# Retention in 64-position chunks with 64x64 quarters in place of 128-position chunks

## The chip, the cores and the metric

The kernel runs on one core of one Trainium2 chip. The metric is device time in microseconds (us) of one launch. TensorE (PE) multiplies, VectorE (DVE), ScalarE (ACT) and GpSimd (POOL) work elementwise, SyncE (SP) issues the DMAs in program order. Each engine takes its instructions in the order in which they stand; only semaphores tie the engines together. Matmul results land in PSUM; here every PSUM tile is one bank (128 partitions x 512 float32).

## The reference

Four batches, 768 positions, 8 heads of 64 channels. A retention (linear attention with a decay per head) feeds a gated MLP:

```
gamma = 1.0 - 2.0 ** (-5.0 - np.arange(H))
for t in range(S):
    state = gamma[None, :, None, None] * state + np.einsum('bhd,bhe->bhde', k[:, :, t], v[:, :, t])
    y[:, :, t] = scale * np.einsum('bhd,bhde->bhe', q[:, :, t], state)

h = np.maximum(x @ w_in, 0.0)                 # x: y as (4, 768, 512), w_in 512 x 1024
u, v = (h[..., :d_ff // 2], h[..., d_ff // 2:])
v_n = (v - mean(v)) / np.sqrt(var(v) + 1e-06)
v_s = np.einsum('ts,bsd->btd', w_spatial, v_n) + b_spatial[None, :, None]
return (u * v_s) @ w_out                      # w_out 512 x 512
```

The weights `w_in` and `w_out` arrive in double precision.

## The kernel before

**MLP.** All its products are formed from operands that are split into a rounded high part and a remainder, three matmuls on the full 128x128 array for one product (`split3`, L316, and L414). For a batch: `mlp_v` (six tiles `v`, then `mlp_norm`), then eight items, each `mlp_u` (tile `u`), `mlp_spatial` (tile `sp`, which needs all six normalised tiles `vnh`, `vnl` of the batch) and `mlp_out` (tiles `o`). Weights are split on chip, block by block (`split_double`, tiles `da`, `df`: five DVE steps, two ACT, the rest DVE or POOL).

**Retention.** 24 chunks of 128 positions, six for a batch, numbered `g` through all batches (`c` is the place in the batch). Values are multiplied by a falling power of gamma (`scale_v`, POOL, L211), outputs by a rising one (`qd_t`, DVE, L279). `run(g)` does three things:

- `ret_out`: tile `x`, for each of four head pairs two matmuls of values on scores (L261: 128 rows of contraction, 64 columns of weights, 128 moving columns) and, from the second chunk of a batch, two of state on queries (L264, 64 rows). So the form of the matmul changes at every pair of heads.
- `score(g + 1)`: the scores of the next chunk. Chunks 0 to 8 (`scores_whole`, L244) form them from float32 operands and mask them on DVE (L248). Chunks 9 to 23 (`scores_split`, L224) use split operands stacked to 128 rows (`stack`: DVE, ACT and POOL work, L118, L202, L206), add two halves (L226 ACT, L227 DVE) and mask on POOL (L228).
- `ret_update`: tile `u`, keys on values (L289); the sum with the old state on DVE (L298), its decay on POOL (L299).

A float32 matmul shows in the profile as two passes, that of a split operand as one.

**Order.** The lists START, FIRST, REST and LAST give the order in which the parts are issued: START holds the splits of the weights, the whole first batch's retention (R0 to R5), R6 to R8 of the second batch, and the first `v` tiles; FIRST the items of batch 0 and R9 to R11; REST the items of a batch and the six chunks of the next batch; LAST the last eight items. A planner then sets each engine's order from these parts and from the pools: a tile of a pool can be written only when the tile that held its buffer is done with. The retention's PSUM pool has three banks for `s`, `x` and `u`.

Of the kernel before, what the change touches and what calls it, by code (L numbers as in the profile page):

```python
# [22 lines left out]
WHOLE = 9  # L23
# [7 lines left out]
START = (  # L31
# [3 lines left out]
)  # L35
FIRST = (
    "C7 L10 I0 L11 W01 W11 W21 C8 I1 W31 C9 I2 W51 T12 C10 W41 R9 T11 I3 C11 I4 Q11 R10 "
    "Q12 I5 I6 Q13 R11 V0 I7 V1 N0 V3 V2 N1 N2 T13 N3 V5 V4 N4 N5 O7"
)
REST = (  # L40
    "R0 Q2 T2 R1 I0 I1 Q3 T3 I2 R2 Q4 T5 I3 I4 R3 T4 Q5 I5 R4 Q6 T6 I6 Q7 T7 V0 I7 R5 V1 "
# [5 lines left out]
# Order in which the blocks of the weights in double precision are split, and how many of the  # L47
# residues are formed on the vector engine.
# [7 lines left out]
def tile_retention_gmlp(  # L56
    ctx: ExitStack,
    tc: tile.TileContext,
    qk: bass.AP,
    qT: bass.AP,  # L60
    kT: bass.AP,
    kv: bass.AP,
# [8 lines left out]
    cdecay: bass.AP,  # L71
# [5 lines left out]
    NG = kv.shape[0]  # L77
    NC = NG // B
    H, D = kv.shape[3], kv.shape[4]
    NP = H // 2  # L80
# [16 lines left out]
    mask_t = wpool.tile([P, P], F32, name="mask_t")  # L97
    vd_t = wpool.tile([P, H], F32, name="vd_t")
    qd_t = wpool.tile([P, NP, P], F32, name="qd_t")
    cd_t = wpool.tile([P, NP], F32, name="cd_t")  # L100
# [38 lines left out]
    def split_double(i):  # L139
# [3 lines left out]
        a = mpool.tile([P, DM], F32, tag="stage", name=f"da{i}")  # L143
# [19 lines left out]
    query = {}  # L163
    keys = {}
    kvs = {}
    stacked = {}
    scores = {}
    state = {}
    xhalf = {}

    def load_query(g):
        if g >= NG:
            return
        if g < WHOLE:
            t = rpool.tile([P, 2, NP, P], F32, tag="qk", name=f"qk{g}", bufs=3)
            load(t, qk[g])
            query[g] = [t[ROWS[h % 2], 0, h // 2] for h in range(H)]
            keys[g] = t[:, 1]
        else:
            kt = rpool.tile([P, NP, P], F32, tag="qk", name=f"k{g}", bufs=3)  # L180
            qt = rpool.tile([P, H, P], F32, tag="qk", name=f"q{g}", bufs=3)
            load(kt, kT[g - WHOLE])
            load(qt, qT[g - WHOLE])
            query[g] = [qt[ROWS[h % 2], h] for h in range(H)]
            keys[g] = kt
            stack(g, kt, qt)

    def load_value(g):
        if g >= NG:
            return  # L190
        kvs[g] = rpool.tile([P, 2, H, D], F32, tag="kv", name=f"kv{g}")
        load(kvs[g], kv[g])
        scale_v(g)

    def stack(g, kt, qt):
        k2 = mpool.tile([P, H, P], F32R, tag="raw", name=f"k2_{g}", bufs=3)
        q2 = [
            mpool.tile([P, NP, 2, P], F32R, tag="raw", name=f"q2_{g}_{i}", bufs=3)
            for i in range(2)
        ]  # L200
        for r in range(2):
            nc.scalar.copy(k2[ROWS[r], r::2], kt[ROWS[r]])  # L202
            residue(nc.vector, k2[ROWS[1 - r], r::2], kt[ROWS[r]], k2[ROWS[r], r::2])
        for i in range(2):
            qi = qt[:, NP * i : NP * i + NP]
            nc.scalar.copy(q2[i][:, :, 0], qi)  # L206
            residue(nc.gpsimd, q2[i][:, :, 1], qi, q2[i][:, :, 0])
        stacked[g] = (k2, q2)

    def scale_v(g):  # L210
        nc.gpsimd.tensor_tensor(  # L211
            kvs[g][:, 1], kvs[g][:, 1], vd_t[:, :].unsqueeze(2).broadcast_to([P, H, D]), ALU.mult
        )

    def scores_split(g):
        k2, q2 = stacked.pop(g)
        ps = []
        for i in range(2):
            p = rpool.tile([P, NP, P], F32, tag="p", name=f"p{g}_{i}", bufs=3)
            for u in range(2):  # L220
                t = ps_r.tile([P, 2, 2, P], F32, tag="ret", name=f"s{g}_{i}_{u}")
                for w in range(2):
                    h = 2 * u + w
                    nc.tensor.matmul(t[:, w], k2[:, NP * i + h], q2[i][:, h], start=True, stop=True)  # L224
                low = rpool.tile([P, 2, P], F32, tag="low", name=f"lo{g}_{i}_{u}")
                nc.scalar.copy(low, t[:, :, 1])  # L226
                nc.vector.tensor_tensor(p[:, 2 * u : 2 * u + 2], t[:, :, 0], low, ALU.add)  # L227
            nc.gpsimd.affine_select(  # L228
                out=p,
                in_=p,  # L230
                pattern=[[0, NP], [1, P]],
                compare_op=ALU.is_ge,
                fill=0.0,
                base=0,
                channel_multiplier=-1,
            )
            ps.append(p)
        scores[g] = [ps[h // NP][:, h % NP] for h in range(H)]

    def scores_whole(g):  # L240
        ts = [ps_r.tile([P, NP, P], F32, tag="ret", name=f"s{g}_{r}") for r in range(2)]
        for h in range(H):
            r, hp = h % 2, h // 2
            nc.tensor.matmul(ts[r][:, hp], keys[g][ROWS[r], hp], query[g][h], start=True, stop=True)  # L244
        ps = []
        for r in range(2):
            p = rpool.tile([P, NP, P], F32, tag="p", name=f"p{g}_{r}", bufs=3)
            nc.vector.tensor_tensor(  # L248
                p, ts[r], mask_t[:, :].unsqueeze(1).broadcast_to([P, NP, P]), ALU.mult
            )  # L250
            ps.append(p)
        scores[g] = [ps[h % 2][:, h // 2] for h in range(H)]

    def ret_out(g):
        b, c = divmod(g, NC)
        ps = scores.pop(g)
        t = ps_r.tile([P, NP, P], F32, tag="ret", name=f"x{g}")
        for hp in range(NP):
            for r in range(2):
                h = 2 * hp + r  # L260
                nc.tensor.matmul(t[ROWS[r], hp], kvs[g][:, 1, h], ps[h], start=True, stop=(c == 0))  # L261
            if c > 0:
                for r in range(2):
                    nc.tensor.matmul(  # L264
                        t[ROWS[r], hp],
                        state[g][ROWS[r], hp],
                        query[g][2 * hp + r],
                        start=False,
                        stop=True,
                    )  # L270
# [8 lines left out]
        nc.vector.tensor_tensor(xf, t, qd_t, ALU.mult)  # L279
        nc.scalar.copy(xh[:, :, cols], xf)  # L280
        residue(nc.gpsimd, xl[:, :, cols], xf, xh[:, :, cols])

    def ret_update(g):
        c = g % NC
        if c == NC - 1:
            return
        t = ps_r.tile([P, 4, P], F32, tag="ret", name=f"u{g}")
        for h in range(H):
            nc.tensor.matmul(  # L289
                t[ROWS[h % 2], h // 2, :D], kvs[g][:, 0, h], kvs[g][:, 1, h], start=True, stop=True  # L290
            )
        st = rpool.tile([P, NP, D], F32, tag="st", name=f"st{g}")
        cd = cd_t[:, :].unsqueeze(2).broadcast_to([P, NP, D])
        if c == 0:
            nc.vector.tensor_tensor(st, t[:, :, :D], cd, ALU.mult)
        else:
# [243 lines left out]
```

## Time and profile before

| | |
|---|---|
| median of 3 runs | 451.26 us (450.74 to 451.58) |
| span of the profiled execution | 445.8 us; the runs are some 5.5 us longer than it, which lies around the span |
| PE, DVE, POOL, ACT busy | 429.1, 234.2, 217.6, 159.8 us |
| matmul passes | 2834, 1288 of them in the retention |
| first `sp` matmul of batch 0 | at 81.16 us |
| data moved by DMA | 45.23 MB |

A row of the PE timeline merges passes of one line; its start, set against the start of the next row, gives the time that the passes took, since the ends are modelled and overlap.

### The profile page before, as it was taken

To read this page: it belongs to the slowest core of one execution; us is meant where nothing else is said; L and a number is where in the kernel's file an instruction comes from. 1 tells how busy PE (TensorE), PEld (TensorE's weight loads), DVE (VectorE), ACT (ScalarE), POOL (GpSimd) and SP (SyncE) were. 2 spreads that over 40 slices of the span, in tenths; PEclk is the share of its full clock that TensorE was granted. 3 is DMA by queue.
4 is the path that set the end of the run, shared out by engine and by line. 5 is a ranking of instruction groups with operands and counts; after the bars stand their busy time and mean duration, and the time that the engine had idled before them with its cause. 6 is when DMAs were issued, how large, how long until landed. Compare 5 with 4: busy or idle time off the path is not lost.

```text
span 445.8 us, 7214 instructions
## 1 busy us (share of the span) xinstructions
PE 429.1 (96%) x2834; PEld 352.0 (79%) x2834; DVE 234.2 (53%) x397; ACT 159.8 (36%) x319; POOL 217.6 (49%) x228
## 2 busy tenths in 40 slices
PE   4998989989999999999999999999999999999995
PEld 2665657777899877887988877888879778999994
DVE  2899989883863556661423556652413534422122
ACT  2324234543434344641433433652423312411211
POOL 1457874695673627473724747365534522211110
PEclk8899999996999999999999999999999999999999
DMA  7846456434125320530213330342313000100102
GB/s 259 312 129 217 130 192 216 147 132 131 43 101 190 93 73 0 209 123 1 96 71 130 109 118 0 102 160 71 96 71 119 1 0 2 71 1 0 72 0 71
DMA packets 16881, 45.23 MB, mean 101 GB/s; under 512 B 2128, under 2 KB 4048, under 8 KB 16848
## 3 DMA queue, kind: packets, MB, share of 16 engines
q1 hardware_dynamic: 16848, 44.77, 29.7%
q8 instruction: 22, 0.36, 0.3%
q14 instruction: 11, 0.09, 0.1%
HBM read 38.48 MB, written 6.29 MB: 100 GB/s over the span
## 4 chain that ended last, share of the span: by engine, by line
PE 77%; DVE 10%; POOL 5%; issue 3%; DMA 3%; SPq 1%; ACT 0%; ACTq 0%; POOLq 0%; DVEq 0%
PE sp L316 22%; PE o L414 14%; PE u L316 14%; PE v L316 11%; PE x L261 6%; PE x L264 5%; PE s L224 3%; PE u L289 2%; DMA kv<-in_kv_dram 1%; DVE p L248 1%; DVE df L149 1%; DMA k<-in_kT_dram 1%; DVE da L151 1%; DVE da L147 1%; DVE da L150 1%
## 5 line engine op out<-in xcount | busy, mean ns | idle before, releaser
L118 POOL TENSOR_TENSOR gl<-t,gh 128x384 fp32r<-128x384 f32 x31 | 32.0, 1032 | 76.2 <-ACT gh L400 72.5
L316 PE MATMUL sp<-wsp_h,vnh 128*128 128x384 f32 x192 | 65.4, 341 | 0.0
L316 PE MATMUL sp<-wsp_l,vnh 128*128 128x384 f32 x192 | 65.0, 339 | 0.0
L316 PE MATMUL sp<-wsp_h,vnl 128*128 128x384 f32 x192 | 64.3, 335 | 0.0
L398 DVE TENSOR_TENSOR t<-sp,bsp_t 128x384 f32<-128x384 f32 (+1 forms) x34 | 17.9, 532 | 76.7 <-PE sp L316 74.3
L261 PE MATMUL x<-p,kv 128*64 128x128 f32 x384 | 45.0, 306 | 6.4 <-POOL kv L211 4.4
L118 POOL TENSOR_TENSOR xl<-xf,xh 128x512 fp32r<-128x512 f32 x24 | 35.0, 1460 | 25.5 <-ACT xh L280 23.3
L118 POOL TENSOR_TENSOR q<-q,q 128x512 fp32r<-128x512 f32 x30 | 41.1, 1380 | 11.9 <-ACT q L206 11.9
L316 PE MATMUL u<-xh,winu_h 128*128 128x384 f32 x128 | 43.9, 343 | 0.0
L261 PEld LDWEIGHTS x<-p,kv 128*64 128x64 f32 x384 | 22.0, 140 | 27.4 <-issue 19.1
L316 PE MATMUL u<-xh,winu_l 128*128 128x384 f32 x128 | 43.5, 340 | 0.0
L316 PE MATMUL u<-xl,winu_h 128*128 128x384 f32 x128 | 43.1, 337 | 0.0
L400 ACT CAST gh<-t 128x384 fp32r<-128x384 f32 (+1 forms) x34 | 16.6, 494 | 68.9 <-DVE t L399 67.8
L316 PE MATMUL v<-winv_h,xh 128*128 128x512 f32 x96 | 39.3, 411 | 0.0
L316 PE MATMUL v<-winv_h,xl 128*128 128x512 f32 x96 | 39.0, 406 | 0.0
L227 DVE TENSOR_TENSOR p<-s,lo 128x256 f32<-128x256 f32 x60 | 23.8, 419 | 28.5 <-ACT lo L226 28.3
L316 PE MATMUL v<-winv_l,xh 128*128 128x512 f32 x96 | 38.7, 404 | 0.0
L211 POOL TENSOR_TENSOR kv<-kv,vd_t 128x512 f32<-128x512 f32 x24 | 26.9, 1120 | 24.0 <-DMA kv<-in_kv_dram 17.9
L228 POOL TENSOR_SCALAR_AFFINE_SELECT p<-p 128x512 f32<-128x512 f32 x30 | 24.2, 808 | 28.8 <-DVE p L227 28.6
L414 PE MATMUL o<-wout_l,gh 128*128 128x512 f32 x96 | 37.5, 394 | 0.0
L316 PEld LDWEIGHTS sp<-wsp_h,vnh 128*128 128x128 f32 x192 | 36.0, 188 | 1.7 <-issue 0.7
L226 ACT COPY lo<-s 128x256 f32<-128x256 f32 x60 | 21.0, 374 | 45.6 <-PE s L224 40.3
(73 smaller groups left out, 878.6 us busy)
## 6 DMA issues: line engine op xcount, KB each, us to landing
kv<-in_kv_dram SPq DMA_DIRECT2D x24, 512.0 KB, 3.5
q<-in_qT_dram SPq DMA_DIRECT2D x15, 512.0 KB, 3.4
out_dram<-ot SPq DMA_DIRECT2D x23, 256.0 KB, 2.0
qk<-in_qk_dram SPq DMA_DIRECT2D x9, 512.0 KB, 5.4
k<-in_kT_dram SPq DMA_DIRECT2D x15, 256.0 KB, 3.6
wst<-in_w_sp_dram SPq DMA_DIRECT2D x12, 192.0 KB, 3.6
raw<-in_w_inv_dram SPq DMA_DIRECT2D x4, 512.0 KB, 6.6
raw<-in_w_inu_dram SPq DMA_DIRECT2D x4, 512.0 KB, 3.8
```

The costliest lines, as they stand in the source:

```text
L118: eng.tensor_tensor(out, whole, high.bitcast(F32), ALU.subtract)
L211: nc.gpsimd.tensor_tensor(kvs[g][:, 1], kvs[g][:, 1], vd_t[:, :].unsqueeze(2).broadcast_to([P, H, D]), ALU.mult)
L224: nc.tensor.matmul(t[:, w], k2[:, NP * i + h], q2[i][:, h], start=True, stop=True)
L226: nc.scalar.copy(low, t[:, :, 1])
L227: nc.vector.tensor_tensor(p[:, 2 * u : 2 * u + 2], t[:, :, 0], low, ALU.add)
L228: nc.gpsimd.affine_select(out=p, in_=p, pattern=[[0, NP], [1, P]], compare_op=ALU.is_ge, fill=0.0, base=0, channel_multiplier=-1,)
L261: nc.tensor.matmul(t[ROWS[r], hp], kvs[g][:, 1, h], ps[h], start=True, stop=(c == 0))
L264: nc.tensor.matmul(t[ROWS[r], hp], state[g][ROWS[r], hp], query[g][2 * hp + r], start=False, stop=True,)
L316: nc.tensor.matmul(ps, l, r, start=(i == 0), stop=(i == 3 * n - 1))
L398: nc.vector.tensor_tensor(t[:, c], pp[:, c], bsp_t[:, tc_], ALU.add)
L400: nc.scalar.copy(gh[:, c], t[:, c])
L414: nc.tensor.matmul(o, l[:, col], r[:, j], start=(j == 0 and n == 0), stop=(j == NJ - 1 and n == 2))
```

## The change

Chunks of 128 positions are still loaded as one, but are worked as two halves `i` of 64 positions (`C = 64`).

- **Layout.** Queries land in tile `m` (`pq`) in two pieces, for the two heads `r` of each pair on opposite halves of the partitions; masked scores are later written into the other halves of the same tile. Values land likewise in `w` (`vs`), states in its other halves. So values lie on top of the state, and scores on top of the queries, as 128-row operands.
- **`ret_out`**: one matmul of 128 rows (`w` on `m`) for a head and a half, 64 moving columns, in place of the pair L261 and L264.
- **`score`, `ret_update`**: each matmul is 64 rows by 64 columns by 64 moving columns, in one quarter of the array; the loops go through the four quarters in turn. Each fills two PSUM tiles, `s{g}_0`, `s{g}_1` and `u{g}_0`, `u{g}_1`. The split scores (`stack`, `scores_split`) are gone.
- **State unscaled.** Powers of gamma count through the whole batch, so the state needs no decay (L299 is gone); it is added up per half chunk on DVE, in four pieces of 64 x 256 for a chunk (ACT copies the first two of a batch), and scores are masked in four such pieces.
- **Loads.** The rising powers differ by chunk, so 256 KB of them (`qd`) are loaded for every chunk; a chunk has seven loads (`q` two, `kT`, `v` two, `k`, `qd`) where it had two, or three from chunk 9. Values are scaled in two instructions of 64 x 512.
- **Order.** `run(g)` is now update, scores of `g + 1`, output. In START some R stand one or two places later, after the loads of the next chunks. The splits' tile `da` now takes buffers of tag `xf`.

```diff
 START = (
-    "Q0 v m L0 q T0 c Q1 L1 T1 L2 Z R0 Q2 L3 T2 Q3 C0 C1 L4 R1 T3 L5 C2 C3 L6 R2 Q4 T4 V0 "
-    "R3 C4 Q5 T5 V1 N0 L7 R4 V3 W10 Q6 T6 V2 W00 R5 Q7 T7 N1 N2 C5 L8 W40 W20 B W30 R6 Q8 "
+    "Q0 v m L0 T0 Q1 L1 T1 L2 Z R0 Q2 L3 T2 Q3 C0 C1 L4 R1 T3 L5 C2 C3 L6 Q4 T4 R2 V0 "
+    "C4 Q5 T5 R3 V1 N0 L7 R4 V3 W10 Q6 T6 V2 W00 R5 Q7 T7 N1 N2 C5 L8 W40 W20 B W30 Q8 "
...
+    def score(g):
...
+        for hp in range(NP):
+            for i in range(2):
+                for r in range(2):
+                    col = r if i == 0 else 1 - r
+                    nc.tensor.matmul(
+                        ts[i][ROWS[col], hp, :C],
+                        kt[ROWS[1 - r], i, hp],
+                        m[ROWS[1 - r], r, i, hp],
...
+        for i in range(2):
+            for r in range(2):
...
+                nc.vector.tensor_tensor(m[ROWS[r], r, i], ts[i][col, :, :C], mk, ALU.mult)
...
+    def ret_update(g):
...
+                    nc.tensor.matmul(
+                        ts[i][ROWS[col], hp, :D],
+                        kn[ROWS[r], i, hp],
+                        w[ROWS[r], r, i, hp],
...
+                dst = w[ROWS[1 - r], r, 1] if i == 0 else values[g + 1][ROWS[1 - r], r, 0]
+                if g % NC == 0 and i == 0:
+                    nc.scalar.copy(dst, u)
+                else:
+                    nc.vector.tensor_tensor(dst, u, w[ROWS[1 - r], r, i], ALU.add)
...
     def ret_out(g):
-            for r in range(2):
-                h = 2 * hp + r
-                nc.tensor.matmul(t[ROWS[r], hp], kvs[g][:, 1, h], ps[h], start=True, stop=(c == 0))
-            if c > 0:
-                for r in range(2):
-                    nc.tensor.matmul(
-                        t[ROWS[r], hp],
-                        state[g][ROWS[r], hp],
-                        query[g][2 * hp + r],
+                    rows = ROWS[r] if c == 0 and i == 0 else slice(0, P)
+                    nc.tensor.matmul(
+                        t[ROWS[r], hp, i],
+                        w[rows, r, i, hp],
+                        m[rows, r, i, hp],
...
     def run(g):
+        ret_update(g)
+        score(g + 1)
         ret_out(g)
-        score(g + 1)
-        ret_update(g)
```

**A late chunk on PE.** Before, the output of chunk 11 and the first scores of chunk 12 (`x`, `p` scores, `kv` values, `q` queries, `st` state; `v` is MLP):

```order
L316 MATMUL v1_1_1632<-winv_h_80,xl6_642 128x512
L261 MATMUL x11_1524<-p11_0_1350,kv11_1191 64x128 x2
L264 MATMUL x11_1524<-q11_1315,st10_1387 64x128 x2
L261 MATMUL x11_1524<-p11_0_1350,kv11_1191 64x128 x2
L264 MATMUL x11_1524<-q11_1315,st10_1387 64x128 x2
L261 MATMUL x11_1524<-p11_1_1364,kv11_1191 64x128 x2
L264 MATMUL x11_1524<-q11_1315,st10_1387 64x128 x2
L261 MATMUL x11_1524<-p11_1_1364,kv11_1191 64x128 x2
L264 MATMUL x11_1524<-q11_1315,st10_1387 64x128 x2
L224 MATMUL s12_0_0_1546<-q2_12_0_1396,k2_12_1395 128x256 x2
L224 MATMUL s12_0_1_1552<-q2_12_0_1396,k2_12_1395 128x256 x2
```

Now, the scores of chunk 17 and the output of chunk 16:

```order
L279 MATMUL u1_3_1_2738<-xl9_1424,winu_h_80 128x384
L201 MATMUL s17_0_2681<-pq17_2601,kt17_2602 64x64 x8
L279 MATMUL u1_3_1_2738<-xh9_1423,winu_l_81 128x384
L279 MATMUL u1_3_1_2738<-xh9_1423,winu_h_80 128x384
L279 MATMUL u1_3_1_2738<-xl9_1424,winu_h_80 128x384
L201 MATMUL s17_1_2682<-pq17_2601,kt17_2602 64x64 x8
L248 MATMUL x16_2703<-pq16_2402,vs16_2407 64x64 x16
L279 MATMUL u1_3_1_2738<-xh9_1423,winu_l_81 128x384
```

The eight changes between L261 and L264 are one block of 16 matmuls. The scores often stand as two blocks of eight, one for a tile, each of which uses two of the four quarters; where they alternate (`s_0` twice, `s_1` twice, and so on) all four follow each other.

**The first `sp` on PE.** Before, it stands behind the update of chunk 7, with the output of chunk 8 in pieces between its passes:

```order
L316 MATMUL u0_1_0_921<-xh0_144,winu_l_83 128x384
L289 MATMUL u7_737<-kv7_597 64x64 x8
L316 MATMUL sp0_0_0_936<-wsp_h_84,vnh0_338 128x384
L261 MATMUL x8_813<-p8_0_733,kv8_674 64x128
L316 MATMUL sp0_0_0_936<-wsp_l_85,vnh0_338 128x384
```

Now:

```order
L201 MATMUL s9_0_1088<-pq9_928,kt9_929 64x64 x8
L201 MATMUL s9_1_1089<-pq9_928,kt9_929 64x64 x8
L248 MATMUL x8_1110<-pq8_822,vs8_827 64x64 x16
L224 MATMUL u9_0_1362<-vs9_937,kn9_938 64x64 x5
L224 MATMUL u9_1_1363<-vs9_937,kn9_938 64x64 x4
L224 MATMUL u9_0_1362<-vs9_937,kn9_938 64x64
L224 MATMUL u9_1_1363<-vs9_937,kn9_938 64x64 x2
L224 MATMUL u9_0_1362<-vs9_937,kn9_938 64x64 x2
L224 MATMUL u9_1_1363<-vs9_937,kn9_938 64x64 x2
L201 MATMUL s10_0_1384<-pq10_1052,kt10_1053 64x64 x8
L279 MATMUL sp0_0_0_1174<-wsp_h_82,vnh0_448 128x384
```

All of chunk 8, the update of chunk 9 and half of the scores of chunk 10 moved ahead of the first `sp`.

**The same place on DVE.** Before (`vnl` ends the normalisation of batch 0, `xf8` the output of chunk 8, `da8` is the ninth block of weights):

```order
L248 TENSOR_TENSOR p8_0_733<-s8_0_723,mask_t_73 128x512
L118 TENSOR_TENSOR vnl0_339<-vr0_5_785,vnh0_338 128x512
L248 TENSOR_TENSOR p8_1_735<-s8_1_724,mask_t_73 128x512
L118 TENSOR_TENSOR wsp_l_85<-wst5_0_765,wsp_h_84 128x384
L149 SCALAR_TENSOR_TENSOR df8_977<-raw8_617,da8_976 128x512
L298 TENSOR_TENSOR sm7_747<-u7_737,st6_670 128x256
L150 TENSOR_SCALAR da8_976<-df8_977 128x512
L151 SCALAR_TENSOR_TENSOR da8_976<-raw8_617,da8_976 128x512
```

Now:

```order
L238 TENSOR_TENSOR vs8_827<-u8_0_1066,vs8_827 64x256 x2
L145 TENSOR_SCALAR da6_1039<-df6_1040 128x512
L238 TENSOR_TENSOR vs9_937<-u8_1_1067,vs8_827 64x256 x2
L146 SCALAR_TENSOR_TENSOR da6_1039<-raw6_367,da6_1039 128x512
L212 TENSOR_TENSOR pq9_928<-s9_0_1088,mask_t_73 64x256 x2
L212 TENSOR_TENSOR pq9_928<-s9_1_1089,mask_t_73 64x256 x2
L263 TENSOR_TENSOR xf8_1127<-x8_1110,qd8_832 128x512
L142 TENSOR_SCALAR da7_1131<-da7_1131 128x512
```

When `xf8` is formed, the splits stand at the seventh block (`da6`) instead of the ninth; the masks and the state's additions are pairs of 64 x 256.

More of the change, by code (lines that the diff above doesn't have):

```diff
@@ L70, in tile_retention_gmlp @@
     qdecay: bass.AP,
-    cdecay: bass.AP,
     out: bass.AP,
@@ L95, in tile_retention_gmlp @@
     ps_o = ctx.enter_context(tc.tile_pool(name="ps_o", bufs=3, space=bass.MemoryType.PSUM))
[L97 to L100, printed above, removed]
+    mask_t = wpool.tile([P, C], F32, name="mask_t")
+    vd_t = wpool.tile([P, NC, 2, NP], F32, name="vd_t")
     bsp_t = wpool.tile([P, S], F32, name="bsp_t")
@@ L161, in split_spatial @@
         residue(pick(c + NC * half < VECTOR_SPATIAL), wsp_l[:, c, cols], st, wsp_h[:, c, cols])
-    query = {}
+    queries = {}
     keys = {}
[L165 to L168, printed above, removed]
+    naturals = {}
+    values = {}
+    decays = {}
     xhalf = {}
@@ L173, in load_query @@
             return
[L174 to L186, printed above, removed]
+        m = rpool.tile([P, 2, 2, NP, C], F32, tag="pq", name=f"pq{g}", bufs=3)
+        kt = rpool.tile([P, 2, NP, C], F32, tag="kt", name=f"kt{g}", bufs=2)
+        for r in range(2):
+            load(m[ROWS[1 - r], r], q_in[g, ROWS[1 - r]])
+        load(kt, kT[g])
+        queries[g], keys[g] = m, kt
     def load_value(g):
@@ L210, in scale_v @@
[L210 to L245, printed above, removed]
-        for r in range(2):
[L247 to L252, printed above, removed]
+        w = rpool.tile([P, 2, 2, NP, D], F32, tag="vs", name=f"vs{g}", bufs=3)
@@ L254, in ret_out @@
     def ret_out(g):
         b, c = divmod(g, NC)
[L256 to L262 removed]
+        m, w = queries.pop(g), values.pop(g)
+        t = ps_r.tile([P, NP, 2, C], F32, tag="ret", name=f"x{g}")
+        for i in range(2):
+            for hp in range(NP):
```

137 lines of the change are left out of this document (67 added, 70 removed), and 2 rows, old and new, of the table START.

## The prediction

> **What bounds the kernel now.** First the page's slices, to see which engine is full where:
>
> ```profile
> PE 429.1 (96%) x2834; PEld 352.0 (79%) x2834; DVE 234.2 (53%) x397; ACT 159.8 (36%) x319; POOL 217.6 (49%) x228
> PE   4998989989999999999999999999999999999995
> DVE  2899989883863556661423556652413534422122
> PEclk8899999996999999999999999999999999999999
> ```
>
> Then the busy times by stretch (columns: stretch, its length; busy time of PE, weight load, DVE, ACT, POOL with instructions; clock; DMA):
>
> ```profile
> 8.50:65.30 56.80, 49.68 (x412) 33.73 (x412) 54.33 (x84) 17.33 (x29) 37.55 (x35) 0.91 0.58 200
> 65.30:90.40 25.10, 25.10 (x213) 18.66 (x212) 21.87 (x36) 11.76 (x24) 15.81 (x17) 1.00 0.60 201
> 90.40:110.00 19.60, 17.91 (x125) 13.62 (x125) 12.87 (x18) 8.06 (x17) 14.22 (x13) 0.83 0.37 112
> 110.00:445.80 335.80, 331.03 (x2063) 283.69 (x2061) 144.81 (x259) 120.67 (x248) 149.70 (x161) 1.00 0.22 74
> ```
>
> There are two regimes. From 8.5 to about 90 us DVE is busy 76.2 of 81.9 us and sets the pace; PE has few passes for its busy time and a lowered clock. From 110 us on PE is full at full clock and the others have half their time free. So each PE microsecond saved in the second regime counts, and in the first only what DVE must do. The border is the first `sp`, which needs all of batch 0's normalised tiles. Here are the PE rows that give my prices (start, length, passes):
>
> ```profile
> 21.02 1.16 PE L244 MATMUL s<-qk 64*128 64x128 f32 x16
> 22.11 0.50 PE L316 MATMUL v<-winv_h,xh 128*128 128x512 f32 x1
> 27.32 1.16 PE L244 MATMUL s<-qk 64*128 64x128 f32 x8
> 28.41 0.69 PE L289 MATMUL u<-kv 128*64 128x64 f32 x16
> 81.16 0.44 PE L316 MATMUL sp<-wsp_h,vnh 128*128 128x384 f32 x1
> 85.72 0.40 PE L224 MATMUL s<-q,k 128*128 128x256 f32 x2
> 85.95 0.34 PE L316 MATMUL u<-xl,winu_h 128*128 128x384 f32 x1
> 93.34 0.33 PE L316 MATMUL sp<-wsp_h,vnl 128*128 128x384 f32 x1
> 93.52 0.34 PE L316 MATMUL sp<-wsp_h,vnh 128*128 128x384 f32 x1
> 93.78 0.69 PE L289 MATMUL u<-kv 128*64 128x64 f32 x16
> 94.40 0.44 PE L316 MATMUL sp<-wsp_l,vnh 128*128 128x384 f32 x1
> 94.68 0.34 PE L316 MATMUL sp<-wsp_h,vnl 128*128 128x384 f32 x1
> 208.57 0.44 PE L261 MATMUL x<-p,kv 128*64 128x128 f32 x4
> 208.94 0.44 PE L264 MATMUL x<-q,st 64*64 64x128 f32 x4
> 209.30 0.44 PE L261 MATMUL x<-p,kv 128*64 128x128 f32 x4
> ```
>
> Sixteen score passes that alternate between the two row halves take 1.09 us (21.02 to 22.11); eight that stay in one half take the same 1.09 (27.32 to 28.41). So passes in different halves run two abreast. Sixteen passes of 64 columns take 0.62 (93.78 to 94.40), 0.47 less than sixteen of 128: 0.030 us for a pass of 64 columns two abreast, 0.059 for 128. An `sp` pass is 0.18 (93.34 to 93.52); from 93.52 to 94.68 there are two of them and the block, so the block costs 1.16 - 0.36 = 0.80, of which 16 x 0.030 = 0.48 is work: a way in and out of the full-array form is some 0.33, or 0.17 a change. Four passes of `x` take 0.37 (208.57 to 208.94), of which 4 x 0.059 is work: a change between L261 and L264 is 0.13. A split score pass is 0.115 (85.72 to 85.95).
>
> **PE from the first `sp` on.** I counted both orders from there. The MLP passes are the same 1440. Retention before: 480 passes of `x` x 0.059 = 28.3; 120 split score passes x 0.115 = 13.8; 208 of `u` x 0.030 = 6.2; 80 changes to or from the full array x 0.17 = 13.6; 93 among the small forms x 0.13 = 12.1. Sum 74.0 us. After: 480 passes of `x` x 0.030 = 14.4; 432 of scores and 400 of updates x 0.030 = 25.0; 94 changes x 0.17 = 16.0; 15 x 0.13 = 2.0. Sum 57.4: **16.6 us less** if quarters run two abreast. Of the 832 quarter passes, 392 stand where all four quarters follow each other; four abreast they cost half, 5.9 less: **22.5 us less**. No row shows four abreast; halves of rows (L244) and of columns (L289) each run abreast, and a quarter is one of each, so I take 22. Of this, work moved ahead of the first `sp` is part: it is now done while PE has time to spare.
>
> [...] This case's rows show two abreast only.
>
> **DVE up to the first `sp`.** That is the cost side. In the new order `sp` stands behind half of chunk 10's scores, whose PSUM buffer comes free only with `xf8`. So I compare DVE's list up to `xf8`:
>
> ```profile
> L118 DVE TENSOR_TENSOR k<-k,k 64x512 fp32r<-64x512 f32 x30 | 26.0, 867 | 13.3 <-ACT k L202 12.5
> L227 DVE TENSOR_TENSOR p<-s,lo 128x256 f32<-128x256 f32 x60 | 23.8, 419 | 28.5 <-ACT lo L226 28.3
> L248 DVE TENSOR_TENSOR p<-s,mask_t 128x512 f32<-128x512 f32 x18 | 12.0, 678 | 0.8 <-PE s L244 0.8
> L151 DVE SCALAR_TENSOR_TENSOR da<-raw,da 128x512 f32<-128x512 uint32 x12 | 12.9, 1072 | 0.1
> L149 DVE SCALAR_TENSOR_TENSOR df<-raw,da 128x512 int32<-128x512 int32 x12 | 10.5, 876 | 1.3 <-POOL wout_l L154 1.2
> L147 DVE TENSOR_SCALAR da<-da 128x512 f32<-128x512 f32 x12 | 8.1, 675 | 9.9 <-ACT da L146 9.9
> L148 DVE TENSOR_SCALAR da<-da 128x512 int32<-128x512 int32 x12 | 7.2, 599 | 0.1
> L150 DVE TENSOR_SCALAR da<-df 128x512 int32<-128x512 int32 x12 | 6.9, 575 | 0.1
> L298 DVE TENSOR_TENSOR sm<-u,st 128x256 f32<-128x256 f32 x16 | 6.6, 416 | 0.8 <-PE u L289 0.8
> 89.67 0.69 DVE L279 TENSOR_TENSOR xf<-x,qd_t 128x512 f32<-128x512 f32 x1 [0.87 <-PE x L264]
> ```
>
> Added: 40 masks and 30 additions of 64 x 256. No row has that shape; 128 x 256 from PSUM takes 0.416 (L298), and half the partitions need not be cheaper (64 x 512 takes 0.867, no less than the 0.678 of 128 x 512); so 0.416 rather than half of it, and 70 x 0.416 = 29.1. Gone: 18 masks (12.2), 7 state steps (2.9), two key remainders (1.7), two additions of score halves (0.8), the first `sp`'s two gate steps (1.3), and two of nine splits, which come later, at 0.675 + 0.599 + 0.876 + 0.575 + 1.072 = 3.8 each (7.6). Sum 26.5. So `xf8` comes 2.6 later than the 90.4 of before, on a DVE that idles only some 5 us until then.
>
> The start adds to it. The first output began when POOL had scaled the values:
>
> ```profile
> 11.04 2.27 PE L261 MATMUL x<-p,kv 128*64 128x128 f32 x16 [4.38 <-POOL kv L211]
> L211 POOL TENSOR_TENSOR kv<-kv,vd_t 128x512 f32<-128x512 f32 x24 | 26.9, 1120 | 24.0 <-DMA kv<-in_kv_dram 17.9
> GB/s 259 312 129 217 130 192 216 147 132 131 43 101 190 93 73 0 209 123 1 96 71 130 109 118 0 102 160 71 96 71 119 1 0 2 71 1 0 72 0 71
> ```
>
> Values now come before keys and powers, 0.5 MB earlier in the queue (1.8 us at some 290 GB/s), but are scaled in two steps (+1.1), and the update, its copies and the next scores stand ahead of the first output (some 1 us each). DVE's next splits stand behind that in its order: between +1 and +4, I take +2. The first `sp` is then at 95, between 91 (the old `xf8`, nothing lost) and about 106.
>
> Hidden: the extra 256 KB per chunk and the five extra issues (DMA is 0.6 busy there, and 0.2 later); POOL's second scaling, 24 x 1.12 = 27 us more, against decay, masks and query remainders removed; ACT's work, which only shrinks. If that cover goes, the late loads land in the start, which is the first rival.
>
> **After the first `sp`** five splits are still to be done where before three were, and `u` needs two of them at once. Before, 97.9 to 109.6 held 6.8 us of matmuls in 11.7 (clock 0.83): 5 lost. I take 8 lost there, +3, between 0 and +8.
>
> **Sum.** Before, the first `sp` is at 81.2 and 364.6 follow. After: 95 + 364.6 - 22 + 3 = 440.6 span, against 445.8. With the 5.5 around the span that the median of 451.26 shows: **446 us**. By two abreast it would be 451.
>
> **Rivals.**
> 1. *The start slips further: slower.* SP issues in order. The load of weight block 8 waits until DVE is done with block 5; behind it stand spatial weights that DVE needs six rows later, and behind those chunk 8's five loads. The rule is already visible:
>
> ```profile
> SPq L115 <- DVE da L151: 15.2, 4, 6.0
> ```
>
> Up to 6.0 us a time. Two such waits in a row put the first `sp` at 106: 106 + 364.6 - 20 + 3 = 453.6, or 459 us. It decides from 100 on (445.8 - 364.6 + 22 - 3). Against it: the same wait stood in the old order and DVE stayed full.
> 2. *The start costs almost nothing:* first `sp` at 90, nothing lost to the splits: 90 + 364.6 - 22.5 = 432, or 438 us.
> 3. *Quarters run in single file.* Both row halves now write the same PSUM bank. But L264's passes do that already (heads on opposite halves, one `x` bank), and four of them take the 0.37 of L261's. In single file 832 passes cost 0.030 more each: 440.6 + 25 + 5.5 (nothing four abreast) = 471, or 477 us. [...]
> 4. *It cancels:* the start loses what the rest gains, within 0.2% (0.9 us, about what a measurement can tell here).
>
> **Chances.** Forecast, first `sp` from 91 to 99 (442 to 450 us): 0.45. Rival 1: 0.29. Rival 2: 0.13. Rival 3: 0.04. Rival 4: 0.09. Faster 0.58, same 0.09, slower 0.33. The range 433 to 463 leaves out rival 3, the lower quarter of rival 2 and the upper part of rival 1. The forecast's own range is 442 to 450.
>
> **What would show it.** `x` blocks of 32 passes in about 1.1 us; update and score blocks of 32 in 0.6 to 1.1; DVE rows of 64 x 256 at 0.42; the first `sp` at 95 and 346 us or less from there to the end; PE rows waiting for splits just after it. Wrong I would be if the first `sp` came after 100, if quarter blocks took 2 us, or if waits on PSUM buffers appeared on PE after 130.

## The result and the profile after

The changed kernel takes **477.91 us** (median of 4 runs, 477.32 to 480.45) against 451.0 us of the kernel before in the same comparison: ratio **1.062 (95% interval 1.058 to 1.067)**, slower, where 446 was forecast. The profiled execution has a span of 475.5 us. The page's busy times, slices and clock:

```profile
PE 412.8 (87%) x3786; PEld 354.3 (75%) x3786; DVE 235.1 (49%) x445; ACT 110.9 (23%) x207; POOL 162.3 (34%) x176
...
PE   4567649654399989999999999999999999999995
...
DVE  1769655854976744546414343656143525521112
...
PEclk8666668796679999999999999999999999999999
```

Then the same stretches as before the change (stretch, length; busy PE, weight load, DVE, ACT, POOL; clock, DMA share, GB/s):

```profile
8.50:65.30 56.80, 31.84 (x424) 23.39 (x426) 38.07 (x69) 10.45 (x18) 24.38 (x23) 0.66 0.64 174
65.30:90.40 25.10, 19.94 (x254) 15.52 (x251) 17.13 (x35) 7.81 (x14) 11.56 (x15) 0.77 0.54 153
90.40:110.00 19.60, 12.93 (x155) 11.01 (x155) 12.02 (x24) 4.51 (x8) 6.00 (x7) 0.76 0.45 140
```

DVE, busy 54.3 of 56.8 us in the first of them before, is now busy 38.1: the start has not become too much work, it waits. How much of the loss lies there is read by cutting at a point behind which nearly the same work is left in every order, the first `sp` of the second batch. Before, at 184.20 us:

```profile
0.00:184.20 184.20, 172.32 (x1218) 132.40 (x1218) 133.23 (x210) 71.68 (x137) 110.31 (x111) 0.95 0.44 148
184.20:445.80 261.60, 256.83 (x1620) 219.62 (x1616) 100.96 (x188) 88.09 (x183) 107.26 (x117) 1.00 0.20 69
```

After, at 226.00, with the first `sp` of all, at 132.07, as a cut too:

```profile
0.00:132.07 132.07, 78.66 (x1034) 59.67 (x1034) 86.55 (x160) 29.51 (x51) 51.23 (x56) 0.72 0.59 162
132.07:226.00 93.93, 90.77 (x723) 79.36 (x721) 54.51 (x92) 27.06 (x52) 40.32 (x42) 0.98 0.28 88
226.00:475.50 249.50, 243.36 (x2034) 215.27 (x2032) 94.02 (x194) 54.30 (x104) 70.73 (x79) 1.00 0.24 71
```

From the second batch on the change wins 261.6 - 249.5 = **12.1 us**; up to there it loses 226.0 - 184.2 = **41.8 us**. The difference, 29.7 us, is that of the two spans; the medians differ by 26.9, because the profiled execution of before was some 3 us quicker than its median, and every comparison with its trace below can be too large by that much. What SP waited for (us in all, times, longest), up to the first `sp` at 132:

```profile
SPq L110 <- DVE da L146: 51.8, 7, 10.7
SPq L110 <- DVE xf L263: 15.5, 2, 11.6
```

The wait for `da`'s last step, which frees a raw weight block, was 15.2 us in the whole kernel before. One turn of it in the timeline of after, rows of DVE, SP and PE:

```profile
52.19 0.69 DVE L146 SCALAR_TENSOR_TENSOR da<-raw,da 128x512 f32<-128x512 uint32 x1
...
87.58 0.68 DVE L263 TENSOR_TENSOR xf<-x,qd 128x512 f32<-128x512 f32 x1
...
88.27 0.39 DVE L142 TENSOR_SCALAR da<-da 128x512 f32<-128x512 f32 x1
...
96.89 0.87 DVE L146 SCALAR_TENSOR_TENSOR da<-raw,da 128x512 f32<-128x512 uint32 x1
...
97.33 0.44 PE L279 MATMUL u<-xh,winu_h 128*128 128x384 f32 x1
...
97.81 0.33 SPq L110 DMA_DIRECT2D raw<-in_w_out_dram  x1
98.19 0.90 SPq L110 DMA_DIRECT2D wst<-in_w_sp_dram  x2
...
104.05 1.11 SPq L110 DMA_DIRECT2D pq<-in_q_dram  x2
...
131.03 1.12 PE L201 MATMUL s<-pq,kt 64*64 64x64 f32 x16 [4.70 <-DVE vs L238]
132.07 0.69 PE L279 MATMUL sp<-wsp_h,vnh 128*128 128x384 f32 x1
```

Block 4's split ends at 52; block 5's starts only right behind the output of chunk 5 (`xf`, 87.58). Its end frees a raw buffer, and in the same microsecond SP goes on, with spatial weights and the loads of chunk 8 behind. Block 5 also holds the weights of the first MLP tile `u`, which comes at 97.33 instead of 68.1 before.

The same binding stands at the very start, in the DVE rows of the timeline of after:

```profile
13.75 0.88 DVE L238 TENSOR_TENSOR vs<-u,vs 64x256 f32<-64x256 f32 x2 [5.61 <-ACT vs L236]
14.96 1.75 DVE L212 TENSOR_TENSOR pq<-s,mask_t 64x256 f32<-64x256 f32 x4 [0.33 <-PE s L201]
16.90 0.69 DVE L263 TENSOR_TENSOR xf<-x,qd 128x512 f32<-128x512 f32 x1 [0.19 <-PE x L248]
17.51 1.29 DVE L142 TENSOR_SCALAR da<-da 128x512 f32<-128x512 f32 x1
```

Before, the first split began at 8.5, while DVE waited for chunk 0. Now it stands behind chunk 0's output.

### The profile page after: what moved, and what is told of

Its sections match the earlier page's. It is cut to its first block, busy times and chain, and to the rows that moved or that the text cites. A ratio compares the mean times of both kernels' runs of the same rounds, so it can differ in the third digit from the quotient of the medians.

```text
span 475.5 us, 9213 instructions
## 1 busy us (share of the span) xinstructions
PE 412.8 (87%) x3786; PEld 354.3 (75%) x3786; DVE 235.1 (49%) x445; ACT 110.9 (23%) x207; POOL 162.3 (34%) x176
## 4 chain that ended last, share of the span: by engine, by line
PE 57%; DMA 16%; DVE 9%; POOL 6%; SPq 4%; issue 3%; ACT 2%; ACTq 0%; POOLq 0%
PE sp L279 16%; PE o L377 12%; PE v L279 12%; PE u L279 9%; DMA vs<-in_v_dram 9%; DMA wst<-in_w_sp_dram 5%; SPq L110 4%; POOL vs L188 3%; PE s L201 3%; PE x L248 3%; DMA kt<-in_kT_dram 3%; PE u L224 2%; DVE da L146 1%; DVE vs L238 1%; POOL xl L113 1%
## 5 line engine op out<-in xcount | busy, mean ns | idle before, releaser
L188 POOL TENSOR_TENSOR vs<-vs,vd_t 64x512 f32<-64x512 f32 x48 | 51.1, 1065 | 100.2 <-DMA vs<-in_v_dram 88.5
L201 PE MATMUL s<-pq,kt 64*64 64x64 f32 x768 | 33.9, 252 | 32.3 <-DVE vs L238 13.7
L113 POOL TENSOR_TENSOR gl<-t,gh 128x384 fp32r<-128x384 f32 x31 | 31.3, 1009 | 89.3 <-ACT gh L363 89.0
L201 PEld LDWEIGHTS s<-pq,kt 64*64 64x64 f32 x768 | 28.3, 160 | 41.9 <-issue 23.1
L212 DVE TENSOR_TENSOR pq<-s,mask_t 64x256 f32<-64x256 f32 x96 | 40.4, 421 | 23.2 <-PE s L201 21.6
L238 DVE TENSOR_TENSOR vs<-u,vs 64x256 f32<-64x256 f32 x80 | 33.8, 422 | 20.7 <-PE u L224 13.1
L279 PE MATMUL v<-winv_h,xh 128*128 128x512 f32 x96 | 42.6, 445 | 0.9 <-ACT winv_h L147 0.9
L113 POOL TENSOR_TENSOR xl<-xf,xh 128x512 fp32r<-128x512 f32 x24 | 31.6, 1316 | 31.5 <-ACT xh L266 30.7
L224 PEld LDWEIGHTS u<-vs,kn 64*64 64x64 f32 x704 | 20.4, 148 | 28.1 <-issue 17.4
L224 PE MATMUL u<-vs,kn 64*64 64x64 f32 x704 | 26.8, 244 | 15.4 <-DMA kn<-in_k_dram 7.7
L377 PE MATMUL o<-wout_h,gl 128*128 128x512 f32 x96 | 37.3, 398 | 0.4 <-POOL gl L113 0.3
```

Source lines behind the costliest of these rows:

```text
L113: eng.tensor_tensor(out, whole, high.bitcast(F32), ALU.subtract)
L188: nc.gpsimd.tensor_tensor(w[ROWS[r], r], w[ROWS[r], r], vd, ALU.mult)
L201: nc.tensor.matmul(ts[i][ROWS[col], hp, :C], kt[ROWS[1 - r], i, hp], m[ROWS[1 - r], r, i, hp], start=True, stop=True,)
L212: nc.vector.tensor_tensor(m[ROWS[r], r, i], ts[i][col, :, :C], mk, ALU.mult)
L224: nc.tensor.matmul(ts[i][ROWS[col], hp, :D], kn[ROWS[r], i, hp], w[ROWS[r], r, i, hp], start=True, stop=True,)
L238: nc.vector.tensor_tensor(dst, u, w[ROWS[1 - r], r, i], ALU.add)
```

## The experiments

All times are medians, each with its ratio to the kernel before in the same comparison (449.2 to 450.1 us for the experiments); the other columns are of the profiled executions. "Sixth split" is when DVE begins the last `da` step of the sixth weight block; "second batch" is the first `sp` of that batch, with the time from it to the end.

| kernel | us | ratio (95%) | first `sp` | sixth split | second batch | to the end |
|---|---|---|---|---|---|---|
| before | 451.0 | 1 | 81.2 | 43.6 | 184.2 | 261.6 |
| after | 477.9 | 1.062 (1.058 to 1.067) | 132.1 | 96.9 | 226.0 | 249.5 |
| e1 `da` alone, one buffer | 452.3 | 1.008 (1.005 to 1.011) | 95.4 | 64.4 | 203.6 | 249.0 |
| e2 decays once | 469.9 | 1.048 (1.042 to 1.054) | 125.8 | 92.0 | 220.7 | 247.6 |
| e3 e2 + `da` alone, two | 450.7 | 1.002 (0.998 to 1.005) | 99.4 | 50.4 | 202.1 | 247.4 |
| e4 before + shared | 479.2 | 1.069 (1.062 to 1.075) | 102.6 | 76.7 | 214.4 | 263.9 |
| e5 two factors | 443.9 | 0.985 (0.979 to 0.990) | 93.5 | 45.8 | 196.0 | 245.5 |
| e6 e5 + merged loads | **440.3** | **0.978 (0.974 to 0.982)** | 90.4 | 46.7 | 191.4 | 248.0 |
| e7 before, loads halved | 456.6 | 1.014 (1.010 to 1.019) | 86.9 | 44.2 | 193.7 | 261.3 |
| e8 after, three shared | 467.4 | 1.040 (1.037 to 1.042) | 122.8 | 86.6 | 216.1 | 249.5 |
| e9 e6 + shared | 467.5 | 1.040 (1.037 to 1.044) | 122.4 | 89.8 | 219.1 | 246.8 |
| e10 e6, old start | 442.8 | 0.985 (0.982 to 0.989) | 90.5 | 46.0 | 192.7 | 247.6 |
| e11 e6, three steps to POOL | 445.4 | 0.991 (0.987 to 0.994) | 96.9 | 47.9 | 195.1 | 247.1 |
| e12 e6, two abreast | 449.2 | 0.999 (0.996 to 1.003) | 101.5 | 45.2 | 201.6 | 249.5 |
| e13 after, two splits ahead | 467.6 | 1.037 (1.031 to 1.043) | 118.7 | 89.3 | 217.6 | 249.4 |
| e14 after, seven ahead | 457.6 | 1.015 (1.008 to 1.022) | 114.2 | 58.5 | 206.9 | 249.4 |

### Which edit costs it: e1 to e4

e1 changes one line; e2 takes the decays' load out of the chunk; e3 does both, with two buffers for `da`; e4 puts the change's one line into the kernel before. e2 and e3 leave out each chunk's own power, so they time the work and do not compute the result:

```diff
-        a = rpool.tile([P, DM], F32, tag="xf", name=f"da{i}")
+        a = mpool.tile([P, DM], F32, tag="stage", name=f"da{i}", bufs=1)   # e1; e3: two
-        load(qd, qdecay[g % NC])        # e2, e3: one tile qd_t, loaded once
-        a = mpool.tile([P, DM], F32, tag="stage", name=f"da{i}")           # e4, in before
+        a = rpool.tile([P, DM], F32, tag="xf", name=f"da{i}")
```

> Only the split's work tile `da` changes: it leaves the two buffers that it shares with `xf` and gets one buffer of its own; the decays are still loaded anew for each chunk. Theory A (shared buffers: a block's split has to wait in turn with the chunks' outputs, so its raw weights are freed late, and SP, which issues in order, holds everything behind the next weight load): first `sp` comes from 132 to between 100 and 112, time between 445 and 460 us. Theory B (the decays' load, which waits for `xf` two chunks back, holds SP): first `sp` stays above 125, time 470 to 480. Theory C (more DVE work per chunk sets the pace): unchanged, 475 to 480.

> One set of decays is loaded at the start and used for all chunks, as in the kernel before; the outputs of all chunks but each batch's first then have the wrong scale, the work is otherwise the same. `da` still shares with `xf`. Theory A: first `sp` moves little, stays above 120, time 463 to 476 us. Theory B: the 55 us of waits of the decays' loads go, first `sp` at 100 to 108, time 443 to 453. Theory C: unchanged, 475 to 480.

> Both: decays loaded once (outputs of later chunks in the wrong scale) and `da` in two buffers of its own, as before the change. Theories A and B both expect first `sp` near the 95 of the prediction, 91 to 100, time 438 to 448 us; they differ in how much of it the first two runs have brought already. Theory C (DVE's extra 64x256 steps): first `sp` stays above 115, time above 460.

> The kernel before with one thing of the change only: `da` takes turn with `xf` in two buffers. Theory A: first `sp` goes from 81 to 100 or later, time 468 us or more. Theory B and theory C: within 3 us of the kernel before, 448 to 454.

Theory A holds on both sides: taking `da` out of the shared tag wins 25.6 us (477.9 to 452.3), and sharing alone costs the kernel before 479.2 - 449.2 = 30.0 us, as much as the whole change. Theory C falls: with DVE's 64-row steps unchanged, e1 takes 452.3 us where C expected 475 or more. SP's waits for `da`'s last step shrink with it, in the first 95 us from 30.1 in four waits to 8.6 in one. The decays' load costs 8.0 us while the tag is shared. When it isn't, e3 is 1.6 us below e1 (452.3 to 450.7), but e3 also has a second buffer for `da`, and the two intervals touch; it stays 3 us above the 448 that all theories but C allowed it.

The first `sp` is a poor mark. In e4 it comes at 102.6, and the second batch only at 214.4. In e1 it comes at 95.4, sooner than the 100 to 112 that theory A expected, but with less work ahead of it: 826 matmul passes and 7 outputs, against 1034 passes and 9 outputs in after. The second batch is the better one, with 2036 and 2034 passes from there on: 203.6 in e1, 226.0 in after.

### By which way: e8, e13, e14

```diff
+        ... tag="xf", bufs=3)                                    # e8, both tiles
-    "... Z R0 Q2 L3 T2 Q3 C0 C1 L4 R1 T3 L5 C2 C3 L6 Q4 T4 R2 V0 C4 Q5 T5 R3 ... R5 ... C5 ..."
+    "... Z C0 R0 Q2 L3 T2 Q3 C1 L4 C2 R1 T3 L5 C3 L6 ..."        # e13, e14
+    "... Q4 T4 C4 R2 V0 C5 Q5 T5 R3 V1 N0 L7 C6 R4 ..."          # e14 too
```

> The changed kernel with three buffers in the tag that `da` and `xf` share (as many as in the run with `da` in one buffer of its own, there two and one). Theory A1 (too few buffers): as that run, 450 to 456 us, first `sp` at 95 to 98. Theory A2 (buffers of a tag are handed out in program order, so the first split stands behind the first output on DVE however many there are, and frees its raw block late): raw block 3 is still issued only at 20 us or later, first `sp` at 105 or later, time 460 to 474 us.

> The changed kernel with two words of the start's list moved: the split of block 0 stands ahead of the output of chunk 0, and that of block 2 ahead of the output of chunk 1. Buffers, loads and work are those of the changed kernel. Theory A2 (the turn in which the shared tag is handed out puts the first splits late): the third weight load that has to wait is issued before 16 us instead of 23.7, first `sp` at 110 to 122, time 455 to 468 us, with the rest of the loss left since later splits and outputs still take turns. Theory A3 (waiting for the buffers themselves all through the start, not the first turn): first `sp` stays above 126, time 472 to 480.

> The changed kernel with more words of the start's list moved: the splits of blocks 0 to 6 stand ahead of the outputs of chunks 0 to 4 where they stood behind those of chunks 0 to 8 (blocks 5 and 6 stood behind the outputs of chunks 5 and 8). Buffers, loads and work are those of the changed kernel. Theory A2 (turns of the shared tag are handed out in the list's order): block 5's split ends near 60 us instead of 97 (89 with only the first two moved), first `sp` comes at 96 to 106, time 450 to 459 us. Theory A3 (the two buffers are too few, whoever comes first): the outputs are late instead, first `sp` stays above 112 and the time above 462.

The last `da` step of the splits that began by 100 us, as a group of the timeline (count, shortest, median and longest ns, first and last start). In after, then e13, then e14:

```profile
L146 DVE SCALAR_TENSOR_TENSOR da<-raw,da x6: 678/688/866, 23.0 to 96.9; 128x512 f32<-128x512 uint32 x6
```

```profile
L146 DVE SCALAR_TENSOR_TENSOR da<-raw,da x6: 677/692/1473, 13.7 to 89.3; 128x512 f32<-128x512 uint32 x6
```

```profile
L146 DVE SCALAR_TENSOR_TENSOR da<-raw,da x7: 678/691/1632, 13.5 to 69.2; 128x512 f32<-128x512 uint32 x7
```

A third buffer leaves the first split at 26.0 us and its raw buffer's next load at 26.7. Moving two words brings the split to 13.7 and that load to 17.0 (before 16 was expected), and the sixth split stays late; moving the others brings seven splits by 69 us. So it is the turn, theory A2: a tag's buffers are handed out in the list's order, and in the list block 5's split stands behind chunk 5's output. With buffers of its own it could run ahead of its place, as before. With no buffer and no load changed, the order alone wins 20.3 of the 25.6 us (477.9 to 457.6). e14's first `sp` missed its 96 to 106 and lies where A3 put it, above 112, while the time is A2's; more work stands ahead of it, 1078 passes. Block 7's split, still behind chunk 8 in the list, ends there only at 118, but whether that is why was not tried. The number of buffers counts too: the third one alone wins 10.5 us (477.9 to 467.4), though it leaves the first split late. What is left from e14 to e1 (5.3 us) was not taken apart; A3 can have a part in it.

### The loads: e5, e6, e7, e9

e5 has one set of decays and each chunk's factor per head, and `da` in two buffers of its own; e6 also loads both forms of the keys in one piece, and queries and values of a partition half in one. With this the values come in the queries' place, ahead of the next weight block instead of behind it, and some loads behind the first `sp` change places in the lists. So e6 changes the order of loads as well as their number; e7 changes the number alone. e9 is e6 with `da` back in `xf`.

```diff
+        for hp in range(NP):                                     # e5: xf in four steps
+            nc.vector.scalar_tensor_tensor(
+                xf[:, hp], tx[:, hp], cd_t[:, c, hp : hp + 1], qd_t[:, hp], ALU.mult, ALU.mult
+            )
+        load(k, kk[g])                                           # e6: three loads for a chunk
+        for h in range(2):
+            load(t[ROWS[h], 2 * h : 2 * h + 2], vq[g, ROWS[h]])
-        load(kvs[g], kv[g])                                      # e7, in before; qk alike
+        for i in range(2):
+            load(kvs[g][:, i], kv[g][:, i])
```

> `da` in two buffers of its own; one set of decays loaded once, and each chunk's own factor per head put in on the way from PSUM: `xf` in four 128x128 steps of two multiplications instead of one 128x512 step. It computes what the changed kernel computes, with one load per chunk less. If the sharing was the main loss and the decays' load a small one (1 to 2 us once `da` has buffers of its own), the time is 449 to 454 us, near the run with both, with some 2 us for the longer `xf` steps in the start. If those steps matter on a full DVE, 455 to 460.

> As the run with two factors, and the six loads of a chunk are three: keys in both forms in one of 512 KB, queries and values of each partition half in one of 256 KB. Bytes are the same. Theory D (in the first 30 us SP's issues wait not for buffers but for the loads ahead of them, since only some eight are under way at once, and small ones then leave the memory idle): chunk 1's values land some 4 to 6 us sooner, first `sp` comes from 99 to 91 to 96, time 441 to 447 us. Rival (the start is set by DVE and by buffers, loads are hidden): within 2 us of the run with two factors.

> The kernel before, with each chunk's two loads of 512 KB in the first nine chunks (and all loads of keys and values) issued as two of 256 KB; nothing else. Theory D: the start is later by 3 to 8 us, time 454 to 459 us. Rival (loads are hidden): within 1.5 us of the kernel before, 448 to 452.

> The run with merged loads and two factors, with `da` put back into the two buffers of `xf`. If the shared buffers cost 20 us and more by themselves, whatever the loads: first `sp` above 108, time 458 to 470 us. If they hurt only because seven loads a chunk queue up behind a late weight load: first `sp` below 98, time 440 to 448.

e7 settles that loads are not hidden: the same bytes in twice as many pieces cost the kernel before 6.5 us (456.6 to 450.1). By which way is read from the waits and the rows, and was not tried apart from the issues' own time. SP's order in the changed kernel, loads 7 to 11 (the first eight carry no such wait; `DMAHW0` to `DMAHW7` are the semaphores on which loads report in turn, eight in the trace of after too):

```
L110 DMA vs0_108<-in_v_dram 64x512 x2
L110 DMA kn0_109<-in_k_dram 128x512 [waits DMAHW0_49]
L110 DMA qd0_113<-in_qdecay_dram 128x512 [waits DMAHW1_49]
L110 DMA pq1_117<-in_q_dram 64x512 [waits DMAHW2_49]
```

So here a load is issued only when the eighth before it has landed, and eight small ones are few bytes: by the sizes of the issues, the first eight of after hold 1336 KB, those of before 2374. The semaphores in the trace of after agree: the first weight block lands at 9.13 us and the second, eight loads behind it, is issued at 9.15; chunk 0's values land at 9.86 and chunk 1's are issued at 9.88. Chunk 1's values on SP, and POOL's scaling of chunk 0's and 1's, in the timeline of after:

```profile
9.88 1.12 SPq L110 DMA_DIRECT2D vs<-in_v_dram  x2
...
10.00 2.15 POOL L188 TENSOR_TENSOR vs<-vs,vd_t 64x512 f32<-64x512 f32 x2 [9.19 <-DMA vs<-in_v_dram]
...
16.37 2.15 POOL L188 TENSOR_TENSOR vs<-vs,vd_t 64x512 f32<-64x512 f32 x2 [4.21 <-DMA vs<-in_v_dram]
```

and in that of e6:

```profile
5.37 1.59 SPq L111 DMA_DIRECT2D vq<-in_vq_dram  x2
...
6.80 2.15 POOL L183 TENSOR_TENSOR vq<-vq,vd_t 64x512 f32<-64x512 f32 x2 [5.99 <-DMA vd_t<-in_vdecay_dram]
...
12.83 2.49 POOL L183 TENSOR_TENSOR vq<-vq,vd_t 64x512 f32<-64x512 f32 x2 [3.87 <-DMA vq<-in_vq_dram]
```

The same load in the kernel before, and then in e7:

```profile
5.47 0.67 SPq L115 DMA_DIRECT2D kv<-in_kv_dram  x1
```

```profile
8.41 0.94 SPq L115 DMA_DIRECT2D kv<-in_kv_dram  x2
```

That load is issued 2.9 us later in e7 but lands only 0.8 later, at 14.4 instead of 13.6 by the semaphores. So the rows show that loads wait their turn, and not how 6.5 us come of it. One rival falls: in e7 the smaller pieces were not dearer for the DMA engines, whose packets took 29.7% of 445.8 us before and 29.5% of 455.0 in e7, 132 and 134 us.

The kernel with merged loads beats both: 440.3 us, 2.2% less than before (1.8 to 2.6). Its step over e5 is 3.6 us, more than the rival's 2, though the intervals of the two touch, so it is less sure than e7's 6.5; and it holds the new order of the loads with their smaller number. POOL's scaling of chunk 1's values begins 3.5 us sooner than in e5 (16.33 to 12.83), not the 4 to 6 sooner that its landing was given. Both did better than their expectations, because e5 came out at 443.9 and not at 449 to 454. Why e5 is 6.8 us better than e3 was not found; the second batch begins 6.1 us sooner in it. e9 prices the sharing once more, at 27.2 us, with few loads: the queue of small loads is not what makes it dear.

### What else holds the start: e10, e11, e12

e10 puts the start's list of before into e6; e11 sets `VECTOR_BLOCKS = 2` for 5; e12 turns the loops of scores and updates:

```diff
-        for hp in range(NP):
-            for i in range(2):
+        for i in range(2):
+            for hp in range(NP):
```

> The run with merged loads and two factors, with the start's list in the order of the kernel before (outputs of chunks 2, 6, 7 and 8 ahead of the loads that the change put before them). If the list's new order costs time in the start (the load of a late chunk holds SP or POOL ahead of an output): first `sp` at 84 to 88, time 434 to 438 us. If DVE's work sets the pace by now: within 2 us of the run with merged loads, 438 to 442.

> The run with merged loads and two factors, with three remainders of weight blocks 2 to 4 on POOL instead of DVE: DVE is relieved of three steps of 0.60 us in a stretch where it is busy 54.2 of 56.8 us; POOL gets three of about 1.3. If DVE is now the bound of the start, first `sp` comes 1 to 2 us sooner, time 438 to 440 us; if POOL's chain (scaling, remainders) is as close, 440 to 444.

> The run with merged loads and two factors, with the loops of scores and updates turned: all passes of one PSUM tile, then all of the other, so that at most two quarters of the array are in use at once. If four quarters run abreast, as the block of 32 update passes in 0.63 us against 0.61 for 16 in one tile says, blocks of 32 go from 0.6 to 1.2 us, and from the first `sp` of the second batch to the end the 248 us become 251 to 254; time 442 to 447 us. If blocks of one tile are most of the work anyway, since three PSUM buffers seldom let two tiles start together: within 1.5 us of the 440.25.

The list's new order is not the cost: going back loses 2.6 us (e10), just outside both expectations. e11 fell outside its expectations, at 445.4: what DVE was relieved of was paid back, more than paid; that POOL's chain took it is the reading, not shown. e12 loses 8.9 us, but its stretch from the second batch on only 1.5 (249.5 to 248.0), below the 3 that its first reading wanted. Turning the loops also costs a block less than expected, 0.91 us for 32 update passes where 1.2 was expected and 0.63 is what the changed kernel takes with four abreast:

```profile
199.89 0.98 PE L219 MATMUL u<-vq,kk 64*64 64x64 f32 x32
200.80 0.44 PE L276 MATMUL u<-xh,winu_l 128*128 128x384 f32 x1
```

So the second reading, that blocks of one tile are most of the work anyway, fits the 1.5 us but is not the whole of it. In the profiled executions 10.2 us more lie ahead of the second batch (their spans differ by 11.7); which wait takes them was not settled. In e6 DVE is full again in the start:

```profile
8.50:65.30 56.80, 35.22 (x500) 27.02 (x502) 54.21 (x107) 15.89 (x28) 37.42 (x30) 0.70 0.63 180
```

It still reaches the second batch 7.2 us later than before (191.4 to 184.2). That DVE's added steps are those 7 us is argued from this row, not shown.

## Why the prediction was wrong, point by point

**The step that failed** is the start: "The first `sp` is then at 95", with bounds of 91 and 106. It came at 132.1. The 95 was a sum of DVE's work up to `xf8`, on a DVE assumed to stay full. `xf8` starts at 89.67 before and at 125.53 after; the stretches up to there:

```profile
0.00:89.67 89.67, 79.47 (x646) 54.12 (x647) 75.81 (x120) 31.02 (x54) 52.92 (x54) 0.94 0.60 201
0.00:125.53 125.53, 76.87 (x996) 58.14 (x996) 80.42 (x149) 26.62 (x46) 49.72 (x54) 0.71 0.57 158
```

The work itself was near the sum: DVE is busy 80.4 us instead of 75.8, 4.6 more where 2.6 were forecast. The assumption failed: DVE stands idle for 45.1 us of it, before for 13.9. That e1 has its first `sp` at 95.4 is luck and no support for the 95: `xf8` starts at 113.9 there, behind that `sp`. What the sum left out is an edit that the text ahead of the prediction names and the prediction nowhere prices: `da` moved to the tag of `xf`. It adds no instruction, so a sum of instructions can't see it. It ties each weight split to an output of the retention. DVE's order showed the mark of it, `da6` beside `xf8` where `da8` had stood, and it was taken as a relief, two splits "which come later, at" 3.8 us each.

**Rival 1 had the place.** "The load of weight block 8 waits until DVE is done with block 5; behind it stand spatial weights", and chunk 8's loads: word for word what stands at 96.89 to 104.05. Its size was taken from the old waits (6.0 us) and gave 459. The waits for `da` became 51.8 us in seven turns, because the splits themselves were late. Its point of decision, a first `sp` from 100 on, was right here, but e14 passes it (114.2) with a smaller loss than e4 (102.6): the second batch is the better mark.

**"Hidden: the extra 256 KB per chunk and the five extra issues"** was wrong too. e2 against after gives 8.0 us for the decays, e6 against e5 3.6 for the merging with its new order, and e7 6.5 for pieces in the old kernel. A DMA share of 0.6 says nothing of a start in which each load waits its turn.

**PE's term came out, but not each part of it:** 22 less and 3 given back were forecast from the first `sp` on; measured are 475.5 - 132.1 = 343.4 against 364.6, 21.2 less. PE's busy time there fell from 358.2 us (81.16 to 445.80) to 90.8 + 243.4 = 334.1, by 24.1, and its idle time grew by 2.8. As the forecast said, some of it is work that moved ahead of that mark; from the second batch on the gain is 12.1. Quarters do run abreast, as the PE rows of the timeline of after show:

```profile
74.39 0.68 PE L201 MATMUL s<-pq,kt 64*64 64x64 f32 x16
75.00 1.15 PE L248 MATMUL x<-pq,vs 128*64 128x64 f32 x32
...
96.70 0.69 PE L224 MATMUL u<-vs,kn 64*64 64x64 f32 x32
97.33 0.44 PE L279 MATMUL u<-xh,winu_h 128*128 128x384 f32 x1
```

32 update passes over two tiles take 0.63 us (96.70 to 97.33), 16 score passes of one tile 0.61: four abreast. The 5.9 us that this was given was probably too much: e12 finds 1.5 from the second batch on, and a block of 32 updates takes 0.91 us in it, not twice 0.63. What made up for it was not looked for, so the agreement of the total may be in part luck. The steps of 64 x 256 cost what was said, 0.421 and 0.422 us against 0.416, in the groups of after:

```profile
L212 DVE TENSOR_TENSOR pq<-s,mask_t 64x256 f32<-64x256 f32 x96 | 40.4, 421 | 23.2 <-PE s L201 21.6
L238 DVE TENSOR_TENSOR vs<-u,vs 64x256 f32<-64x256 f32 x80 | 33.8, 422 | 20.7 <-PE u L224 13.1 <-ACT vs L236 5.6
```

**Rival 3** named 477 us, and 477.9 was measured, but by another way: in single file a block of 32 would take 32 x 0.060 = 1.9 us, an estimate with twice the 0.030 of a pass two abreast, and it takes 0.63. In the row of 96.70, 32 passes with rows from both halves went into two PSUM tiles at 0.02 us each.

**The 5.5 us around the span** was too much as well: 477.3 us stand beside the span of 475.5, so 1.8. The 5.5 set the span of one execution of before against the median of others; in a later comparison a run of 447.8 us has a span of 445.7. With that, the prediction's own sum would have been some 442, further off.

## What to carry to other kernels

A tile that changes its tag is a change of order even if no instruction changes: list which tiles share a tag, in the order of the program, and ask what each turn now waits for, and whose load stands behind it on an in-order queue. Where a start is set by loads, count the loads under way and not only the bytes; halving loads lost 6.5 us, and merging six into three, with a new order, won 3.6. To place a loss, cut both traces at a point behind which the work is the same; the first `sp` was no such point, since the planner moved work across it.

## What the runs showed of the hardware that was not expected

With all four 64x64 quarters at work, 32 update passes from both row halves into two PSUM tiles took 0.63 us (96.70 to 97.33); 16 passes of 64 columns, two abreast, took 0.62 before (93.78 to 94.40). Half the partitions did not make a DVE or POOL step much cheaper: a DVE step of 64 x 256 took 0.42 us in after where one of 128 x 256 took 0.416 before, and a POOL scaling of 64 x 512 took 1.07 us where one of 128 x 512 took 1.12. Behind PE's wait of 4.7 us that ends at 131.03 an `sp` pass takes 0.32 us (132.56 to 132.88), against 0.17 before (184.51 to 184.68): the granted clock is 0.50 from 131 to 134 us in after and 1.00 from 183.5 to 187 before, so the work that follows this wait is slower too. The timeline of after:

```profile
132.56 0.52 PE L279 MATMUL sp<-wsp_l,vnh 128*128 128x384 f32 x1
132.88 0.52 PE L279 MATMUL sp<-wsp_h,vnl 128*128 128x384 f32 x1
```

and of before, at a granted clock of 1.00:

```profile
184.51 0.34 PE L316 MATMUL sp<-wsp_l,vnh 128*128 128x384 f32 x1
184.68 0.34 PE L316 MATMUL sp<-wsp_h,vnl 128*128 128x384 f32 x1
```
